# The fifth global transpose moved ahead of the FFN's second product, and other buffers for the last tokens

## The chip, the core and the metric

The kernel runs on one core of one Trainium2 chip. The metric is the device time of one execution in microseconds. Below, PE is TensorE, PEld its weight loads, DVE is VectorE, ACT is ScalarE, POOL is GpSimd and SP is SyncE, which here issues nearly all DMAs. L with a number is a line of the kernel.

## The reference, cut to what matters

Eight batches of eight heads: 512 local tokens attend to a window of 32 tokens on either side and to 32 global tokens; the 32 global tokens attend to all 544. Then a feed-forward network (FFN) over all 4608 tokens.

```python
# batch 8, heads 8, seq_l 512, seq_g 32, head_dim 64; d_model 512, d_ff 2048
s_g = scale * q_g @ [k_g, k_l]^T;  out_g = softmax(s_g) @ [v_g, v_l]
s_l = scale * [q_l @ k_g^T, where(|i-j| <= 32, q_l @ k_l^T, -1e9)]
out_l = softmax(s_l) @ [v_g, v_l]
x = concat(out_g, out_l) as (tokens, heads * head_dim)
h = x @ w_in;  r = max(h, 0);  y = (s * r * r + b) @ w_out
```

## The kernel before, in words

One loop over steps j runs everything as a pipeline. Step j takes one head of one half (256 tokens) of one batch: 16 steps make a batch, 128 steps make the attention. The FFN follows ten steps behind (LAG): with m = j - 10, `ffn_in(m)` makes 256 hidden columns for one tile of 256 tokens (24 matmuls, L508), and `ffn_out(m - 1)` multiplies the result of the step before with `w_out` (12 matmuls, L540, in two halves i = 0 and 1 of six each). Each float32 matrix is held as a high and a low part, so a product is made of three matmuls, and each evacuation from PSUM is a copy on ACT (high part) and a subtraction on DVE (low part).

The order within a step, in program order: split of the next keys and queries, loads, scores of head j (`scores`: L366 for the local ones, L370 for the global rows, then the softmax), transposes of the probabilities of head j - 1 (L312) interleaved with the products of head j - 2 (L391), `x_split` of a finished tile every eighth step, `ffn_in`, the entries of `extra`, and `ffn_out`. From step 20 on (ORDERED) the order on PE is exactly this program order; before it, and on all other engines and the DMA queues throughout, a planner chooses the order from its own estimate of when instructions become ready.

The global tokens: their scores are gathered over a batch in two tiles `sg` of four heads each (group g = 0 and 1). `g_softmax` runs at step 16b + 12 for g = 0 and 16b + 16 for g = 1. Three steps later (16b + 15 and 16b + 19) comes `g_transposes`, here called a turn: five 128x128 transposes of the 544 columns (L439), four into one PSUM tile with tag t and one into a tile with tag g, each followed by a copy on ACT (L442) and a subtraction on DVE (L443) into `pg`. `g_pv` (L460) uses `pg` one and three steps later, and stores its rows to a DRAM buffer `xg_d` (L469).

PSUM tags have one buffer each, so writers wait for the readers of the tile before. Tag t is shared by the probability transposes L312 of every step, the block of four in a turn, and the first transposes of `xg_split`. Tag g is shared by the global scores L370 of every step, the lone fifth transpose in a turn, and `g_pv`.

After the last head, the 256 global rows are the seventeenth tile of tokens: `xg_split(16)`, at m = 127 (step 137), loads them back from `xg_d` in two loads (L488), transposes them (L491) and splits them. Its two load buffers are of tag r, a ring of two that the FFN's hidden tiles `r` (L513) and output tiles `o` (L549) also use.

`ffn_out` is called with the turn as a function `between` and calls it between its two halves.

Of the kernel before, what the change touches and what calls it, by code (L numbers as in the profile page):

```python
# [10 lines left out]
F32 = mybir.dt.float32  # L11
# [9 lines left out]
DM, DF = 512, 2048  # L21
P = 128
HALF = 256
# [7 lines left out]
NC = 416  # L31
# [26 lines left out]
G_TR = 3  # L58
# [6 lines left out]
def f32(ap):  # L65
    return ap.bitcast(F32)
# [3 lines left out]
def window_attention_then_ffn(ctx: ExitStack, tc: tile.TileContext, qd, qg, kw, vw, vg, w_in, w_out, sv, bv, out):  # L70
# [4 lines left out]
    sb = ctx.enter_context(tc.tile_pool(name="sb", bufs=2))  # L75
# [89 lines left out]
    def slot(j):  # L165
        return j // 16, (j // 8) % 2, j % 8
# [66 lines left out]
    def own(k, hf):  # L233
        n, c = (192, P) if hf == 0 else (240, 144)
        return k[:, 0:2 * n].rearrange("p (k c) -> p k c", k=2)[:, :, 0:c]

    def sg_rows(j):
        b, hf, h = slot(j)
        if hf == 0 and h % 4 == 0:
            st_["sg", b, h // 4] = sb.tile([P, SGW], F32, tag=f"sg{h // 4}", name=f"sg{j}", bufs=1)  # L240
        r0 = 32 * (h % 4)
        return st_["sg", b, h // 4][r0:r0 + 32]

    def x_tile(j):
        b, hf, h = slot(j)
        t = 2 * b + hf
        if h == 0:
            xcur[t] = sb.tile([P, 4, HALF], F32, tag="x", name=f"x{t}", bufs=1)
        return xcur[t]

    def load32(j):
        b, hf, h = slot(j)
        if h % 2 == 0:
            if j % 4 == 0:
                rk = sb.tile([P, 480], F32, tag="rk", name=f"rk{j}", bufs=1)
            else:
                rk = sb.tile([P, 10 * D], F32, tag="rvg", name=f"rk{j}", bufs=1)[:, 0:480]
            nc.sync.dma_start(rk[:, 0:NC], kw[b, hf, h // 2])
            st_["rk", j] = st_["rk", j + 1] = rk
        if j % 2 == 0:  # L260
            rq = sb.tile([P, HALF], F32, tag="rq", name=f"rq{j}", bufs=1)
        else:
            rq = sb.tile([P, 288], F32, tag="tg", name=f"rq{j}", bufs=1)[:, 0:HALF]
        nc.sync.dma_start(rq, qd[b, hf, h])
        st_["rq", j] = rq

# [89 lines left out]
    def scores(j):  # L356
        b, hf, h = slot(j)
        ks, qs = st_.pop(("ks", j)), st_.pop(("qs", j))
        p_s = ps.tile([P, 512], F32, tag="s", name=f"ps_s{j}")
        p_g = ps.tile([P, 512], F32, tag="g", name=f"ps_g{j}")  # L360
        qgh = st_["qgs", b][:, h]
        ng = 256 + 32 * hf
        for blk in range(2):
            cols = COLS[hf, blk]
            for a in range(2):
                nc.tensor.matmul(  # L366
                    p_s[:, cols], lhsT=qs[:, a, blk * P:(blk + 1) * P], rhs=ks[:, cols], start=(a == 0), stop=(a == 1),
                )
                if blk == hf and a == 0:
                    nc.tensor.matmul(p_g[0:64, 0:ng], lhsT=qgh, rhs=own(ks, hf), start=True, stop=True)  # L370
        softmax(j, p_s)

        tg = sb.tile([P, 288], F32, tag="tg", name=f"tg{j}", bufs=1)
        nc.scalar.copy(out=tg[0:32, 0:ng], in_=p_g[32:64, 0:ng])  # L374
        nc.vector.tensor_add(out=sg_rows(j)[:, hf * 256:hf * 256 + ng], in0=p_g[0:32, 0:ng], in1=tg[0:32, 0:ng])

# [7 lines left out]
    xcur = {}  # L384
# [47 lines left out]
    def g_transposes(b, g):  # L432
        sg = st_["sg", b, g]
        pg = st_["pg", b, g] = sb.tile([P, 5, 4, 2, SG], F32R, tag="pg", name=f"pg{b}_{g}", bufs=1)
        for c0, c1, tag in ((0, 4, "t"), (4, 5, "g")):
            p_t = ps.tile([P, 4, P], F32, tag=tag, name=f"ps_tg{b}_{g}_{c0}")
            for c in range(c0, c1):
                s0 = min(c * P, SGW - P)
                nc.tensor.transpose(out=p_t[:, c - c0, :], in_=sg[:, s0:s0 + P], identity=ident)  # L439
            v = p_t[:, 0:c1 - c0].rearrange("p c (h q) -> p (c h) q", h=4)  # L440
            ph, pl = (pg[:, c0:c1, :, i, :].rearrange("p c h q -> p (c h) q") for i in range(2))
            nc.scalar.copy(out=ph, in_=v)  # L442
            nc.vector.tensor_sub(out=pl, in0=v, in1=f32(ph))  # L443

    def g_load(b, h):
        rv = sb.tile([P, 10 * D], F32, tag="rvg", name=f"rvg{b}_{h}", bufs=1)
# [37 lines left out]
    def xg_split(t):  # L484
        xs = sb.tile([P, 2, 4, HALF], F32R, tag="xs", name=f"xs{t}", bufs=2)
        for i in range(2):
            xr = sb.tile([P, DM], F32, tag="r", name=f"xgr{i}", bufs=2)
            nc.sync.dma_start(xr, xg_d[i * P:(i + 1) * P, :])  # L488
            p_t = ps.tile([P, 4, P], F32, tag="ts"[i], name=f"ps_xg{i}")
            for c in range(4):  # L490
                nc.tensor.transpose(out=p_t[:, c, :], in_=xr[:, c * P:(c + 1) * P], identity=ident)  # L491
            q = slice(i * P, (i + 1) * P)
            nc.scalar.copy(out=xs[:, 0, :, q], in_=p_t)
            nc.vector.tensor_sub(out=xs[:, 1, :, q], in0=p_t, in1=f32(xs[:, 0, :, q]))
        xs_[t] = xs
# [31 lines left out]

    oacc = {}

    def ffn_out(m, between=None):  # L530
        t, pr = m // 8, m % 8
        g = gs_.pop(m)
        if pr == 0:
            oacc[t] = [ps.tile([P, DM], F32, tag=f"acc{i}", name=f"acc{t}_{i}") for i in range(2)]
        for i in range(2):
            n = 0
            for k in range(2):
                f = 2 * pr + k
                for a, e in ((0, 0), (0, 1), (1, 0)):
                    nc.tensor.matmul(  # L540
                        oacc[t][i], lhsT=g[:, a, k, i * P:(i + 1) * P], rhs=wo[:, e, f, :],
                        start=(pr == 0 and n == 0), stop=(pr == 7 and n == 5),
                    )
                    n += 1
            if i == 0 and between:
                between()
        if pr == 7:
            for i in range(2):
                o = sb.tile([P, DM], F32, tag="r", name=f"o{t}_{i}", bufs=2)  # L549
                nc.scalar.copy(out=o, in_=oacc[t][i])  # L550
                if t < 16:
                    b, hf = t // 2, t % 2
                    r0 = b * (SL + SG) + SG + hf * HALF + i * P
                    nc.sync.dma_start(out[r0:r0 + P, :], o)
                else:
                    rows = out.rearrange("(b r) d -> b r d", r=SL + SG)[4 * i:4 * i + 4, 0:SG, :]
                    nc.sync.dma_start(rows, o)
# [5 lines left out]
    extra, turns = defaultdict(list), {}  # L563
    for b in range(B):
        for g in range(2):
            s0 = 16 * b + G_AT[g]
            extra[s0].append(lambda b=b, g=g: g_softmax(b, g))
            turns[s0 + G_TR] = lambda b=b, g=g: g_transposes(b, g)
            for i in range(2):
                h = 4 * g + 2 * i  # L570
                extra[s0 + G_TR + G_LD[i]].append(lambda b=b, h=h: g_load(b, h))
                extra[s0 + G_TR + G_PV[i]].append(lambda b=b, h=h: g_pv(b, h))
# [22 lines left out]
    for j in range(NM + LAG + 2):  # L595
        if j == ORDERED:
            fixed.enter_context(tc.manual_schedule(engines={mybir.EngineType.PE}))
        sp(j + 1)
        ld(j + 2)
        vl(j)  # L600
        for _ in range(PIECES[j] if j < len(PIECES) else 0):
            weight_piece(piece)
            piece += 1
        if j < NS:
            b1 = j // 16 + 1
            if j == 14 and NF > 16:
                qg_load32(1)
            elif j % 16 == 14 and b1 < B:
                qg_load(b1)
            sc(j)  # L610
            if j == NF - 1 and NF % 16:
                if NF > 16:
                    qg_load(j // 16)
                qg_split(j // 16)
            if j % 16 == 15 and NF <= j + 1 < NS:
                qg_split(b1)
        tr(j - 1)
        transposes_and_pv(j - 1, j - 2)
        vsp(j - 1)
        pvs(j - 2)  # L620
        vl32(j)
        m = j - LAG
        if j % 8 == 1 and 9 <= j <= NS + 1:
            x_split(j // 8 - 1)
        if m == 8 * 16 - 1:
            xg_split(16)
        if 0 <= m < NM:
            ffn_in(m)
        for fn in extra.pop(j, []):
            fn()  # L630
        if 0 <= m - 1 < NM:
            ffn_out(m - 1, turns.pop(j, None))
        elif j in turns:
            turns.pop(j)()
    fixed.close()
    assert piece == 32 and not extra

# [67 lines left out]
```

## Time and profile before

| | us |
|---|---|
| median of 3 runs | 1074.07 (1072.61 to 1075.57) |
| profiled execution | 1072.88 |
| its span, first to last instruction | 1071.1 |
| PE busy | 1031.5 |
| DVE busy | 823.1 |
| ACT busy | 707.4 |

The span is what the profile's views cover; the rest of the execution's time lies around it. A busy engine is not always doing useful work at its peak: matmuls are pipelined and their ends are modelled, so starts are compared below and not ends. Idle time of an engine matters only where it is on the chain that ends last.

### The profile page before, as it was taken

To read this page: it belongs to the slowest core of one execution; us is meant where nothing else is said; L and a number is where in the kernel's file an instruction comes from. 1 tells how busy PE (TensorE), PEld (TensorE's weight loads), DVE (VectorE), ACT (ScalarE), POOL (GpSimd) and SP (SyncE) were. 2 spreads that over 40 slices of the span, in tenths; PEclk is the share of its full clock that TensorE was granted. 3 is DMA by queue.
4 is the path that set the end of the run, shared out by engine and by line. 5 is a ranking of instruction groups with operands and counts; after the bars stand their busy time and mean duration, and the time that the engine had idled before them with its cause. 6 is when DMAs were issued, how large, how long until landed. Compare 5 with 4: busy or idle time off the path is not lost.

```text
span 1071.1 us, 20557 instructions
## 1 busy us (share of the span) xinstructions
PE 1031.5 (96%) x7076; PEld 923.2 (86%) x7076; DVE 823.1 (77%) x2116; ACT 707.4 (66%) x1796; POOL 328.5 (31%) x397
## 2 busy tenths in 40 slices
PE   6989999999999999999999999999999999999896
PEld 2558888999899989999899989998999989999895
DVE  6798778788888878888888888887888878863221
ACT  4677767677777777777667776777677776643221
POOL 3132534234333333234333343233333333211000
PEclk7569999999999999999999999999999999999998
DMA  7665332222222222213222132212221221101000
GB/s 241 192 207 191 97 101 80 67 66 64 90 74 71 64 84 74 76 57 95 67 73 71 58 101 65 76 57 83 88 76 53 79 81 56 59 13 34 21 21 20
DMA packets 63536, 86.80 MB, mean 81 GB/s; under 512 B 7624, under 2 KB 50632, under 8 KB 63432
## 3 DMA queue, kind: packets, MB, share of 16 engines
q1 hardware_dynamic: 63144, 84.44, 25.5%
q8 instruction: 56, 0.92, 0.3%
q10 hardware_dynamic: 288, 1.05, 0.3%
q14 instruction: 48, 0.39, 0.1%
HBM read 76.02 MB, written 9.44 MB: 80 GB/s over the span
## 4 chain that ended last, share of the span: by engine, by line
PE 79%; DVE 11%; ACT 4%; DMA 3%; issue 2%; POOL 0%; SPq 0%; DVEq 0%; ACTq 0%
PE ps_h L508 31%; PE acc L540 30%; PE ps_t L312 4%; PE ps_s L366 4%; PE ps_o L391 4%; DMA wst<-in_w_in 2%; PE ps_og L460 2%; PE ps_g L370 1%; DVE g L523 1%; PE ps_o L328 1%; PE ps_s L282 1%; DVE r L515 1%; DVE x L404 1%; DVE pg L443 1%; DVE sm L227 1%
## 5 line engine op out<-in xcount | busy, mean ns | idle before, releaser
L508 PE MATMUL ps_h<-xs,wi 128*128 128x256 f32 x3264 | 426.0, 286 | 0.0
L508 PEld LDWEIGHTS ps_h<-xs,wi 128*128 128x128 f32 x3264 | 402.2, 190 | 4.8 <-ACT pt L319 0.9
L540 PE MATMUL acc<-wo,g 128*128 128x512 f32 x1632 | 403.6, 393 | 0.9 <-ACT g L522 0.9
L540 PEld LDWEIGHTS acc<-wo,g 128*128 128x128 f32 x1632 | 295.3, 188 | 55.9 <-ACT g L522 1.1
L523 DVE SCALAR_TENSOR_TENSOR g<-r,b_t,g 128x512 fp32r<-128x512 f32 x136 | 118.7, 873 | 72.6 <-ACT g L522 71.9
L522 ACT ACTIVATE g<-r,b_t 128x512 fp32r<-128x512 f32 x136 | 98.5, 724 | 102.8 <-DVE r L515 102.4
L192 POOL TENSOR_TENSOR kq<-rk,kq 64x416 fp32r<-64x416 f32 x56 | 60.9, 1088 | 271.2 <-ACT kq L191 265.6
L515 DVE SCALAR_TENSOR_TENSOR r<-ps_h,s_t,r 128x512 f32<-128x512 f32 x136 | 101.2, 744 | 54.7 <-ACT r L514 54.6
L514 ACT ACTIVATE r<-ps_h 128x512 f32<-128x512 f32 x136 | 81.1, 596 | 93.6 <-PE ps_h L508 86.7
L194 POOL TENSOR_TENSOR kq<-rq,kq 128x256 fp32r<-128x256 f32 x112 | 84.4, 754 | 153.3 <-ACT kq L193 138.0
L220 ACT ACTIVATE sm<-sm,nm 128x224 f32<-128x224 f32 (+1 forms) x256 | 119.6, 469 | 1.7 <-DVE nm L214 1.3
L202 POOL TENSOR_TENSOR vs<-rv,vs 128x256 fp32r<-128x256 f32 x112 | 90.9, 812 | 52.4 <-ACT vs L201 45.8
L214 DVE CUSTOM_DVE_ANT_0 sm<-ps_s,mask 128x224 f32<-128x224 f32 (+1 forms) x256 | 85.6, 370 | 27.4 <-PE ps_s L366 15.4
L312 PE MATMUL ps_t<-ident,sm 128*128 128x128 f32 (+1 forms) x512 | 99.4, 279 | 4.9 <-POOL sm L227 4.8
L391 PE MATMUL ps_o<-pt,vs 128*128 128x256 f32 x448 | 90.6, 284 | 0.0
L374 ACT COPY tg<-ps_g 32x256 f32<-32x256 f32 (+1 forms) x112 | 42.2, 377 | 68.8 <-PE ps_g L370 66.5
L452 POOL TENSOR_TENSOR vsg<-rvg,vsg 128x320 fp32r<-128x320 f32 x64 | 56.3, 900 | 75.1 <-ACT vsg L451 75.1
L366 PE MATMUL ps_s<-kq 128*128 128x192 f32 (+1 forms) x448 | 78.4, 265 | 0.0
L366 PEld LDWEIGHTS ps_s<-kq 128*128 128x128 f32 x448 | 71.9, 189 | 6.8
L402 DVE TENSOR_TENSOR u<-ps_o,u 128x256 f32<-128x256 f32 x112 | 47.4, 423 | 34.0 <-ACT u L401 31.7
L404 DVE TENSOR_TENSOR x<-u 64x256 f32<-64x256 f32 x112 | 69.1, 617 | 3.8
L312 PEld LDWEIGHTS ps_t<-ident,sm 128*128 128x128 f32 (+1 forms) x512 | 59.2, 146 | 13.6 <-POOL sm L227 7.7
(79 smaller groups left out, 1278.1 us busy)
## 6 DMA issues: line engine op xcount, KB each, us to landing
rq<-in_qd SPq DMA_DIRECT2D x128, 128.0 KB, 2.2
rv<-in_vw SPq DMA_DIRECT2D x128, 128.0 KB, 2.0
rk<-in_kw SPq DMA_DIRECT2D x64, 208.0 KB, 2.4
rvg<-in_vg SPq DMA_DIRECT2D x32, 320.0 KB, 2.9
out<-o SPq DMA_DIRECT2D x34, 256.0 KB, 2.0
wst<-in_w_in SPq DMA_DIRECT2D x15, 512.0 KB, 4.7
wst<-in_w_out SPq DMA_DIRECT2D x15, 512.0 KB, 4.6
rqg<-in_qg SPq DMA_DIRECT2D x8, 128.0 KB, 2.5
```

The lines of the kernel that those rows point to most:

```text
L194: nc.gpsimd.tensor_sub(out=qs[:, 1, :], in0=rq, in1=f32(qs[:, 0, :]))
L202: nc.gpsimd.tensor_sub(out=vs[:, :, 1, :], in0=rv4, in1=f32(vs[:, :, 0, :]))
L214: nc.vector.tensor_tensor_reduce(out=sm[:, c], in0=p_s[:, c], in1=mask, op0=ALU.add, op1=ALU.min, scale=-scale, scalar=BIG, accum_out=nm[: ...
L220: nc.scalar.activation(out=p, in_=p, func=AF.Exp, bias=nm[:, blk:blk + 1], scale=-1.0, accum_out=ss[:, blk:blk + 1],)
L312: nc.tensor.transpose(out=p_t[:, at:at + q], in_=sm[0:q, c0:c0 + P], identity=ident[0:q, 0:q])
L366: nc.tensor.matmul(p_s[:, cols], lhsT=qs[:, a, blk * P:(blk + 1) * P], rhs=ks[:, cols], start=(a == 0), stop=(a == 1),)
L391: nc.tensor.matmul(p_o[:, blk, :, q0:q0 + n], lhsT=vs[:, 2 * blk + c], rhs=pt[:, :, o], start=(c == 1), stop=(c == 0),)
L508: nc.tensor.matmul(p_h[:, k], lhsT=wi[:, a, c, f * P:(f + 1) * P], rhs=xs[:, e, c, :], start=(n == 0), stop=(n == 11),)
L515: nc.vector.scalar_tensor_tensor(out=r, in0=p_h, scalar=s_t, in1=r, op0=ALU.mult, op1=ALU.mult)
L522: nc.scalar.activation(out=g[:, 0], in_=r, func=AF.Identity, bias=b_t)
L523: nc.vector.scalar_tensor_tensor(out=g[:, 1], in0=r, scalar=b_t, in1=f32(g[:, 0]), op0=ALU.add, op1=ALU.subtract,)
L540: nc.tensor.matmul(oacc[t][i], lhsT=g[:, a, k, i * P:(i + 1) * P], rhs=wo[:, e, f, :], start=(pr == 0 and n == 0), stop=(pr == 7 and n == 5),)
```

## The change

`g_transposes` becomes a generator with a pause after each of its two blocks, and its blocks change places: first the lone fifth transpose with its copy and subtraction (tag g), then the block of four (tag t). `ffn_out` advances it once ahead of each half. So the fifth transpose now stands between `ffn_in` and `ffn_out`, and the block of four stays between the halves. In `xg_split` the two load buffers are cut from tiles of tag pt (the ring of two for transposed probabilities, 832 columns each) instead of tag r. The tile `x` grows by 24 columns (96 bytes in each partition), and the tiles of tag tg by 40 columns (160 bytes); nothing reads or writes the added columns.

```diff
     def x_tile(j):
...
-            xcur[t] = sb.tile([P, 4, HALF], F32, tag="x", name=f"x{t}", bufs=1)
+            x = sb.tile([P, 4 * HALF + 24], F32, tag="x", name=f"x{t}", bufs=1)
+            xcur[t] = x[:, 0:4 * HALF].rearrange("p (c q) -> p c q", c=4)
...
-            rq = sb.tile([P, 288], F32, tag="tg", name=f"rq{j}", bufs=1)[:, 0:HALF]
+            rq = sb.tile([P, 328], F32, tag="tg", name=f"rq{j}", bufs=1)[:, 0:HALF]
...
-        tg = sb.tile([P, 288], F32, tag="tg", name=f"tg{j}", bufs=1)
+        tg = sb.tile([P, 328], F32, tag="tg", name=f"tg{j}", bufs=1)
...
     def g_transposes(b, g):
...
-        for c0, c1, tag in ((0, 4, "t"), (4, 5, "g")):
+        for c0, c1, tag in ((4, 5, "g"), (0, 4, "t")):
...
             nc.scalar.copy(out=ph, in_=v)
             nc.vector.tensor_sub(out=pl, in0=v, in1=f32(ph))
+            yield
...
     def xg_split(t):
...
-            xr = sb.tile([P, DM], F32, tag="r", name=f"xgr{i}", bufs=2)
+            xr = sb.tile([P, 2 * NC], F32, tag="pt", name=f"xgr{i}")[:, 0:DM]
...
-    def ffn_out(m, between=None):
+    def ffn_out(m, turn):
...
         for i in range(2):
+            next(turn, None)
...
-            if i == 0 and between:
-                between()
...
-            turns[s0 + G_TR] = lambda b=b, g=g: g_transposes(b, g)
+            turns[s0 + G_TR] = g_transposes(b, g)
...
-            ffn_out(m - 1, turns.pop(j, None))
-        elif j in turns:
-            turns.pop(j)()
+            ffn_out(m - 1, turns.pop(j, iter(())))
+        else:
+            list(turns.pop(j, ()))
```

## Rows read from the trace of the kernel before

**Rows 1.** The page's busy line (share of span), and its chain by engine.

```profile
PE 1031.5 (96%) x7076; PEld 923.2 (86%) x7076; DVE 823.1 (77%) x2116; ACT 707.4 (66%) x1796; POOL 328.5 (31%) x397
...
PE 79%; DVE 11%; ACT 4%; DMA 3%; issue 2%; POOL 0%; SPq 0%; DVEq 0%; ACTq 0%
```

**Rows 2.** The table of waits: who waited for whom, us, times, longest.

```profile
PEld ps_g L370 <- DVE pg L443: 10.6, 7, 1.5
...
PE ps_g L370 <- DVE pg L443: 9.7, 13, 1.2
```

**Rows 3.** Timeline, an ordinary step: start, us, engine, line, operation, [idle before <-releaser].

```profile
255.69 0.25 PE L366 MATMUL ps_s<-kq 128*128 128x192 f32 x1
...
255.78 0.28 PE L370 MATMUL ps_g<-kq,qgs 128*64 128x256 f32 x1
...
256.44 0.47 PE L312 MATMUL ps_t<-ident,sm 128*128 128x128 f32 x3
```

**Rows 4.** Timeline, a long turn (step 35) and the next step's scores.

```profile
274.45 1.56 PE L540 MATMUL acc<-wo,g 128*128 128x512 f32 x6
...
275.85 0.77 PE L439 MATMUL ps_tg<-ident,sg 128*128 128x128 f32 x5
...
276.37 1.64 PE L540 MATMUL acc<-wo,g 128*128 128x512 f32 x6
276.96 0.73 ACT L522 ACTIVATE g<-r,b_t 128x512 fp32r<-128x512 f32 x1 [1.67 <-DVE r L515]
277.59 0.73 ACT L442 CAST pg<-ps_tg 128x512 fp32r<-128x512 f32 x2
...
277.72 0.75 DVE L523 SCALAR_TENSOR_TENSOR g<-r,b_t,g 128x512 fp32r<-128x512 f32 x1 [0.79 <-ACT g L522]
277.85 0.25 PE L366 MATMUL ps_s<-kq 128*128 128x192 f32 x1
278.39 0.88 DVE L443 TENSOR_TENSOR pg<-ps_tg,pg 128x512 fp32r<-128x512 f32 x2
...
279.32 0.33 PE L370 MATMUL ps_g<-kq,qgs 128*64 128x256 f32 x1 [1.22 <-DVE pg L443]
...
280.01 0.49 PE L312 MATMUL ps_t<-ident,sm 128*128 128x128 f32 x3
```

**Rows 5.** Timeline, a short turn (step 31) and the next step's scores.

```profile
245.79 0.71 PE L439 MATMUL ps_tg<-ident,sg 128*128 128x128 f32 x5
...
246.42 0.76 ACT L442 CAST pg<-ps_tg 128x512 fp32r<-128x512 f32 x2 [0.90 <-PE ps_tg L439]
...
247.15 0.88 DVE L443 TENSOR_TENSOR pg<-ps_tg,pg 128x512 fp32r<-128x512 f32 x2
...
247.73 0.25 PE L366 MATMUL ps_s<-kq 128*128 128x192 f32 x1
...
248.18 0.31 PE L370 MATMUL ps_g<-kq,qgs 128*64 128x256 f32 x1 [0.20 <-DVE pg L443]
```

**Rows 6.** Groups by line and shape: count, busy us, mean ns, idle before.

```profile
L443 DVE TENSOR_TENSOR pg<-ps_tg,pg 128x512 fp32r<-128x512 f32 x16 | 10.9, 682 | 0.0
...
L443 DVE TENSOR_TENSOR pg<-ps_tg,pg 128x128 fp32r<-128x128 f32 x16 | 4.5, 280 | 0.0
```

**Rows 7.** The chain that ended last, by time: start, us, what.

```profile
1005.10 2.67 DMA xgr<-xg_d
...
1007.81 0.66 PE ps_xg L491 x4
```

**Rows 8.** SP's queue: one wait of the loads, then its timeline from 980 to 1010.

```profile
SPq L488 <- DVE g L523: 6.8, 1, 6.8
...
980.61 11.81 SPq L469 DMA_DIRECT2D xg_d<-xr  x2
999.27 6.17 SPq L488 DMA_DIRECT2D xgr<-xg_d  x2
```

**Rows 9.** One line's matmuls: duration in ns, shortest/median/longest, first and last start.

```profile
L540 PE MATMUL acc<-wo,g x1632: 387/389/504, 95.1 to 1061.7; 128*128 128x512 f32 x182
```

## The prediction

> **What bounds the kernel now.** I read the page's busy line first: PE is busy for 96% of the span, DVE for 77%, ACT for 66% [rows 1]. The chain that ended last is 79% PE [rows 1]. So time can only be won where PE stands still, or by doing fewer matmuls; the change does not alter the number of matmuls. Next I read the table of waits for PE and PEld, and looked only at the names that the diff touches. PE waits 13 times in front of L370, the global scores, for DVE L443: 9.7 us in all. PEld waits at the same place 7 times, 10.6 us, so 1.5 us each [rows 2]; these two rows overlap in time and are not added. Sixteen turns (the steps with global transposes) exist; step 15 lies where the planner still orders PE, and steps 127 and 131 are followed by no scores, which leaves 13: seven long ones (steps 16b+19) and six short ones (16b+15, b from 1). 7 x 1.22 + 6 x 0.20 = 9.7 agrees with [rows 2, 4, 5].
>
> Then the timeline of one ordinary step and one turn of each kind. In the ordinary step the first scores matmul L366 starts at 255.69, L370 at 255.78, and the first transpose of the probabilities, L312, at 256.44: 0.09 and 0.75 us after L366 [rows 3]. After the long turn the same three start at 277.85, 279.32 and 280.01, that is 1.47 and 2.16 us after L366 [rows 4]. The loss is 2.16 - 0.75 = 1.41 us. After the short turn L370 starts 248.18 - 247.73 = 0.45 us after L366, a loss of 0.36 us [rows 5]. Why: bank g holds the fifth transpose, is its turn's last piece of work, and L370 writes the same bank. In the long turn the order on ACT is g (L522) and then both copies L442; on DVE it is g (L523) and then both subtractions L443, ending at 278.39 + 0.88 = 279.27. PE starts 0.05 us later.
>
> **Part 1, the fifth transpose goes first.** It now runs at the place where ffn_out begins, 274.45 in the long turn [rows 4], ahead of six L540, and the other four stay between the halves. No instruction is added or removed: PE has the same matmuls, ACT the same two copies, DVE the same two subtractions, and no DMA is in this part. Bank g's tenant before it, the step's own global scores, was written a whole `ffn_in` of 24 matmuls earlier, so PE should not wait there. The copy of 128 columns is ready for ACT by 275.2 at the latest, even if the one transpose took the 0.71 us of five [rows 5]. Before L522 ACT stands idle for 1.67 us, waiting for DVE L515 [rows 4], so the copy costs nothing. Without that idle it would delay L522 by its own length, under half of the 0.73 us of both copies. The subtraction (0.28 us) is ready before DVE's idle 0.79 us in front of L523 [rows 4], and fits into it; L523 then starts as before. So bank g is free by about 277.3, before L370 wants it at 277.85 + 0.09 = 277.94. That wait goes, by this reading, in all 13 places.
>
> What is late next? Bank t. The block of four keeps its place on all three engines: its copy stands behind L522 and its subtraction behind L523, from 278.39 on. It takes 0.68 us [rows 6] and ends at 279.07; with the 0.05 us above PE may write bank t at 279.12. But the transposes L312 of the next step want that bank at 277.85 + 0.75 = 278.60. So after a long turn PE waits 0.52 us at L312 instead of 1.41 us at L370: the gain is 0.89 us, seven times, 6.2 us. Behind that new wait on PE stand the other transposes, two products L391 and the next 24 L508; ACT L514 waits for these, but no later than it does now. After a short turn the order is the other one: copies ahead of L522 and subtractions ahead of L523, and the block's subtraction is over at 247.15 + 0.68 = 247.83 [rows 5, 6], before 247.73 + 0.75 = 248.48. Nothing takes the place of that wait: 6 x 0.36 = 2.2 us.
>
> Does a lone transpose cost more than one of five? In the turn five L439 last 0.77 us together, and the next L540 starts at 276.37, before they end at 275.85 + 0.77 = 276.62 [rows 4]. In the short turn the five take 0.71 us [rows 5]. So they are pipelined with what follows, and I take nothing for the split. The Trainium skill, page "TensorE: Matmul & The Clock Gate", section "Part 4: PE-mode transpose", gives about 275 ns for one transpose inside a kernel; a transpose that paid this alone, and not 0.71/5 = 0.14 us, would cost 16 x 0.13 = 2.1 us, and the sum by it, as an estimate, would be 9.0 us instead of 11.1. The overlap in these rows speaks against that reading.
>
> **Part 2, the last tokens' buffers.** xg_split reads the 256 global rows back through two buffers. They came from ring r, which the FFN's r and o tiles use; now they come from ring pt, which nobody uses after the last head. The load issued at 999.27 had waited 6.8 us in SP's queue for DVE L523, that is for a buffer of r, although the last store to xg_d was issued by 980.61 + 11.81 = 992.42 [rows 8]. The second load was late: PE stood still from 1005.10 to 1007.81, for that DMA's 2.67 us [rows 7]. From ring pt both loads can be issued once the store has landed; taking 2.67 us for that landing and as much for each load, one behind the other, they are there at 992.42 + 3 x 2.67 = 1000.4, four microseconds before PE asks. They pass nothing in SP's queue: between 992.42 and 999.27 it issues no other transfer. 2.7 us go, with bounds of 0 (loads no earlier) and 2.7 us; I take the upper one, because the wait in the queue is for the buffer and that reason is gone.
>
> **Part 3, two buffers grow.** No instruction reads the added bytes. What changes is where the tiles allocated behind them lie. No row shows what an address is worth, so I bound it by tiles that already rotate through different places: L540 reads g from two buffers, and its shortest and median matmul are 387 and 389 ns [rows 9]. Within 2 ns of 389 that is at most half a percent either way on 403.6 us, some 2 us; I take 0 and keep 2 us to either side. The turns of steps 15 and 19 lie where the planner orders PE too and may place the pieces otherwise; the nearest row is a long turn's loss of 1.41 us, so I keep 2 x 1.41 = 2.8 us to either side and take 0 beyond what is counted above.
>
> **The sum.** 6.2 + 2.2 + 2.7 = 11.1 us. The profiled execution took 1072.88 us, of which 1071.1 are its span; that gives 1061.8. The median of the runs shown is 1074.07, 1.2 us above it, and the forecast is made for a median: 1074.07 - 11.1 = 1063.0 us.
>
> **The rivals.**
> - *Both waits go.* The planner sets the order on ACT and DVE from its own clock. If it puts the block's copy ahead of L522 in the long turns too, as it already does in the short ones [rows 5], bank t is free in time, and the whole 1.41 us is won seven times: 9.9 + 2.2 + 2.7 = 14.8 us, 1059.3. For it: the 1.67 us of idle ACT would take that copy. Against: the block's transposes finish no earlier than before, so what made the planner choose stays.
> - *The orders turn out worse.* If the lone subtraction is put behind L523 (ended 277.72 + 0.75 = 278.47), bank g comes free at 278.75 and t at 279.43: from L366 to L312 1.63 us, a gain of 0.53 us, 3.7 + 2.2 + 2.7 = 8.6 us, 1065.5. If the short turns flip to the long ones' order, their gain becomes a loss of about 0.24 us each: 6.2 - 1.4 + 2.7 = 7.5 us, 1066.6. Against both: the lone piece is ready 1.5 us or more before L522.
> - *The change does not do what it says.* The planner leaves the lone copy behind L522 and its subtraction last, so that only the last tokens' 2.7 us are won: 1071.4, within what can be told from no change. Against: it picks by readiness, as the two kinds of turn show.
> - *Slower, through the addresses.* If the moved tiles made TensorE's reads slower, every one of 3264 + 1632 = 4896 FFN matmuls would pay. 11.1 us / 4896 = 2.3 ns each eat up the gain; from 3.0 ns on the kernel is over 0.3% slower, and 5 ns would give 1074.07 - 11.1 + 24.5 = 1087.5. Against it: the 2 ns spread between shortest and median [rows 9].
>
> **How the numbers follow.** Forecast 0.45, both waits gone 0.22, worse orders 0.15, not what it says 0.10, addresses 0.08. A difference under 0.3%, about 3.2 us, cannot be told from none in measurements of this kernel. Faster by more than that: 0.45 + 0.22 + 0.15 = 0.82; within: 0.10; slower: 0.08. The range goes from the second case less some 2 us for addresses, 1057.5, to 1070.5: the worse orders' 1066.6 with 2 us for addresses and most of the 2.8 us for the early turns. It ends just under the case that wins only the last tokens' wait; that one and the slower one are left out, 0.18 in all.
>
> **What would show each step.** Right: the wait of PE L370 for DVE L443 disappears from the table; a new one, PE or PEld L312 for DVE L443, shows seven times with about half a microsecond each; short turns lose nothing; the two ps_xg groups stand together with no DMA between them in the chain; ordinary steps take what they took. The forecast is wrong if L312 waits for nothing after long turns (then it is nearer 1059), if L370 still waits, if ordinary steps away from the turns become longer, or if the stretch ahead of step 20, where the planner also orders PE, changes its length.

## The result and the profile after

| | before | after |
|---|---|---|
| median of the runs, us | 1074.45 (1072.61 to 1075.57, 4 runs) | 1057.98 (1055.96 to 1059.14, 4 runs) |
| ratio, with its 95% interval | | 0.9846 (0.9825 to 0.9867) |
| span of the profiled execution, us | 1071.1 | 1055.7 |

The changed kernel takes 16.5 us less. 1063.0 was forecast; 1057.98 lies in the stated range, near its lower end.

In the changed kernel the lines below the edits have moved: L508 is now L510 (first product), L540 is L543 (second product), L370 is L371, L312 is L313, L442 and L443 (copy and subtraction of the turn) are L443 and L444, L515 is L517, L522 and L523 (copy and subtraction of g) are L524 and L525.

The page's first line, and its busy line, which answers to [rows 1]:

```profile
span 1055.7 us, 20552 instructions
...
PE 1024.7 (97%) x7076; PEld 918.0 (87%) x7076; DVE 826.2 (78%) x2116; ACT 706.3 (67%) x1796; POOL 329.1 (31%) x397
```

PE has the same 7076 matmuls and is busy for 6.8 us less. That is the first sign of something the forecast does not have: fewer waits shorten the span, but should leave the busy time of the same matmuls as it was.

The table of waits (who waited for whom, us, times, longest), answering to [rows 2]:

```profile
PEld ps_t L313 <- DVE pg L444: 4.1, 7, 0.7
PE ps_t L313 <- DVE pg L444: 2.9, 6, 0.5
...
PEld ps_g L371 <- DVE pg L444: 1.5, 1, 1.5
PE ps_g L371 <- DVE pg L444: 1.2, 1, 1.2
```

Of 13 waits at bank g one is left, and six waits of half a microsecond at bank t have come. The one that is left follows the turn of step 19, ahead of step 20, where the planner orders PE as well.

The long turn of step 35 in the timeline (start, us, engine, line, operation), answering to [rows 4]:

```profile
270.49 3.06 PE L510 MATMUL ps_h<-xs,wi 128*128 128x256 f32 x24
...
273.39 0.27 PE L440 MATMUL ps_tg<-ident,sg 128*128 128x128 f32 x1
...
273.41 1.65 PE L543 MATMUL acc<-wo,g 128*128 128x512 f32 x6
...
274.13 0.26 ACT L443 CAST pg<-ps_tg 128x128 fp32r<-128x128 f32 x1
...
274.90 0.60 PE L440 MATMUL ps_tg<-ident,sg 128*128 128x128 f32 x4
...
275.81 0.28 DVE L444 TENSOR_TENSOR pg<-ps_tg,pg 128x128 fp32r<-128x128 f32 x1
275.92 0.72 ACT L524 ACTIVATE g<-r,b_t 128x512 fp32r<-128x512 f32 x1 [1.53 <-DVE r L517]
276.55 0.57 ACT L443 CAST pg<-ps_tg 128x512 fp32r<-128x512 f32 x1
276.68 0.75 DVE L525 SCALAR_TENSOR_TENSOR g<-r,b_t,g 128x512 fp32r<-128x512 f32 x1 [0.60 <-ACT g L524]
276.73 0.25 PE L367 MATMUL ps_s<-kq 128*128 128x192 f32 x1
276.82 0.28 PE L371 MATMUL ps_g<-kq,qgs 128*64 128x256 f32 x1
...
277.35 0.68 DVE L444 TENSOR_TENSOR pg<-ps_tg,pg 128x512 fp32r<-128x512 f32 x1
...
278.09 0.52 PE L313 MATMUL ps_t<-ident,sm 128*128 128x128 f32 x3 [0.48 <-DVE pg L444]
...
278.69 1.53 PE L510 MATMUL ps_h<-xs,wi 128*128 128x256 f32 x11
```

This is the forecast's picture. The lone copy stands in ACT's idle time (which is 1.53 us and was 1.67), its subtraction in DVE's (0.60 left of 0.79), and L371 starts 0.09 us after L367 instead of 1.47. L313 starts 278.09 - 276.73 = 1.36 us after L367; it was 2.16 before and 0.75 in an ordinary step. It waits for the block of four, behind g on both engines. From one first product to the next this step takes 278.69 - 270.49 = 8.20 us. Before it took 280.57 - 271.52 = 9.05:

```profile
271.52 3.10 PE L508 MATMUL ps_h<-xs,wi 128*128 128x256 f32 x24
...
280.57 3.12 PE L508 MATMUL ps_h<-xs,wi 128*128 128x256 f32 x24
```

The chain that ended last, at the last tokens, answering to [rows 7]:

```profile
993.03 0.87 PE ps_xg L493 x8
```

Eight transposes in one piece, with no DMA between them. The stop is gone.

What the forecast does not have shows best in the last steps, which hold nothing but the FFN: 24 matmuls of the first product, 12 of the second. The chain there, first before, then after (start, us, what):

```profile
1022.59 2.76 PE acc L540 x12
1025.35 2.88 PE ps_h L508 x24
...
1028.23 2.76 PE acc L540 x12
1030.99 2.88 PE ps_h L508 x24
```

```profile
1024.46 2.75 PE acc L543 x12
1027.20 2.80 PE ps_h L510 x24
...
1030.01 2.75 PE acc L543 x12
1032.75 2.80 PE ps_h L510 x24
```

5.64 us a step have become 5.55, with no wait in either. The same 24 matmuls take 0.08 us less, 3 ns each, in steps that no moved instruction touches. The clock is no reason: the granted clock is 1.00, the higher of the two levels (2.4 GHz), in both stretches. Nor are the other engines: while the first product runs from 1025.35 before and from 1027.20 after, ACT and POOL are idle, and DVE is busy for 0.20 and 0.28 us of its time.

### The profile page after: what moved, and what is told of

It reads as the page before. It is cut to its first block, busy times and chain, and to the rows that moved or that the text cites. A ratio compares the mean times of both kernels' runs of the same rounds, so it can differ in the third digit from the quotient of the medians.

```text
span 1055.7 us, 20552 instructions
## 1 busy us (share of the span) xinstructions
PE 1024.7 (97%) x7076; PEld 918.0 (87%) x7076; DVE 826.2 (78%) x2116; ACT 706.3 (67%) x1796; POOL 329.1 (31%) x397
## 4 chain that ended last, share of the span: by engine, by line
PE 81%; DVE 9%; ACT 4%; DMA 2%; issue 2%; POOL 0%; SPq 0%; DVEq 0%; ACTq 0%
PE ps_h L510 32%; PE acc L543 31%; PE ps_t L313 5%; PE ps_s L367 4%; PE ps_o L392 3%; PE ps_og L462 1%; DVE g L525 1%; PE ps_o L329 1%; PE ps_s L283 1%; PE ps_g L371 1%; DMA wst<-in_w_in 1%; DVE x L405 1%; PE ps_g L289 1%; DVE r L517 1%; ACT g L524 1%
## 5 line engine op out<-in xcount | busy, mean ns | idle before, releaser
L510 PE MATMUL ps_h<-xs,wi 128*128 128x256 f32 x3264 | 419.6, 283 | 0.0
L543 PE MATMUL acc<-wo,g 128*128 128x512 f32 x1632 | 405.9, 395 | 0.8 <-ACT g L524 0.8
L510 PEld LDWEIGHTS ps_h<-xs,wi 128*128 128x128 f32 x3264 | 396.2, 189 | 4.8 <-issue 1.0
L543 PEld LDWEIGHTS acc<-wo,g 128*128 128x128 f32 x1632 | 294.8, 188 | 56.9 <-ACT g L524 1.0
L525 DVE SCALAR_TENSOR_TENSOR g<-r,b_t,g 128x512 fp32r<-128x512 f32 x136 | 120.6, 886 | 70.5 <-ACT g L524 70.3
L524 ACT ACTIVATE g<-r,b_t 128x512 fp32r<-128x512 f32 x136 | 98.3, 723 | 103.4 <-DVE r L517 103.2
L517 DVE SCALAR_TENSOR_TENSOR r<-ps_h,s_t,r 128x512 f32<-128x512 f32 x136 | 101.2, 744 | 53.4 <-ACT r L516 53.4
L313 PE MATMUL ps_t<-ident,sm 128*128 128x128 f32 (+1 forms) x512 | 99.6, 279 | 8.0 <-POOL sm L227 5.0
L367 PE MATMUL ps_s<-kq 128*128 128x192 f32 (+1 forms) x448 | 78.0, 265 | 0.0
L367 PEld LDWEIGHTS ps_s<-kq 128*128 128x128 f32 x448 | 71.7, 189 | 6.8
L313 PEld LDWEIGHTS ps_t<-ident,sm 128*128 128x128 f32 (+1 forms) x512 | 59.1, 145 | 17.7 <-POOL sm L227 7.0
L227 DVE TENSOR_SCALAR sm<-sm,ss 128x192 f32<-128x192 f32 (+1 forms) x224 | 68.0, 345 | 1.5
```

Of the source, the lines that this page charges most:

```text
L313: nc.tensor.transpose(out=p_t[:, at:at + q], in_=sm[0:q, c0:c0 + P], identity=ident[0:q, 0:q])
L367: nc.tensor.matmul(p_s[:, cols], lhsT=qs[:, a, blk * P:(blk + 1) * P], rhs=ks[:, cols], start=(a == 0), stop=(a == 1),)
L510: nc.tensor.matmul(p_h[:, k], lhsT=wi[:, a, c, f * P:(f + 1) * P], rhs=xs[:, e, c, :], start=(n == 0), stop=(n == 11),)
L517: nc.vector.scalar_tensor_tensor(out=r, in0=p_h, scalar=s_t, in1=r, op0=ALU.mult, op1=ALU.mult)
L524: nc.scalar.activation(out=g[:, 0], in_=r, func=AF.Identity, bias=b_t)
L525: nc.vector.scalar_tensor_tensor(out=g[:, 1], in0=r, scalar=b_t, in1=f32(g[:, 0]), op0=ALU.add, op1=ALU.subtract,)
```

## The experiments

Where a step's length is given without a row, it is the time from the first matmul of `ffn_in` to that of the next step; "ordinary" is the median over the steps from 31 to 119, "FFN-only" the mean over the last seven. The kernel before has 6.97 us in an ordinary step and 5.64 in an FFN-only one.

**The three parts, one at a time.** Each is the kernel before with one of the edits, or the changed kernel without one:

```diff
 e1_turn:    the changed kernel with
-x = sb.tile([P, 4 * HALF + 24], ...); tg, rq = sb.tile([P, 328], ...); xr = sb.tile([P, 2 * NC], F32, tag="pt", ...)
+x, tg, rq and xr as in the kernel before
 e2_load:    the kernel before with
+xr = sb.tile([P, 2 * NC], F32, tag="pt", name=f"xgr{i}")[:, 0:DM]
 e3_grow:    the kernel before with
+x = sb.tile([P, 4 * HALF + 24], ...); tg, rq = sb.tile([P, 328], ...)
 e4_nogrow:  the changed kernel with
-x = sb.tile([P, 4 * HALF + 24], ...); tg, rq = sb.tile([P, 328], ...)
+x, tg and rq as in the kernel before
```

Expected of e1_turn:

> Part 1 alone: the fifth transpose goes first; buffers and the last tokens' loads as before. Theory A (each part is worth what its own stretch shows, and the rest of the gain belongs to the buffers' addresses): 6 long turns x 0.86 and 6 short ones x 0.43, that is 7.7 us less than before; ordinary steps keep 6.94 us, FFN-only steps 5.64. Theory B (the turns are worth more than they show, since the relieved ACT and DVE speed up the ordinary steps behind them): 12 to 13 us less, and ordinary steps become shorter.

Expected of e2_load:

> Part 2 alone: the last tokens' rows are loaded into ring pt. Both theories: the 3.0 us stop between the two transposes of the last tokens goes, nothing else moves: 3 us less than before.

Expected of e3_grow:

> Part 3 alone: the two buffers grow, so the tiles behind them move by 160 bytes and, from r on, by 256; the instructions are those of before in the same order on every engine. Theory A: 4 to 5 us less, spread evenly over all steps (FFN-only steps 5.64 to 5.55 us, the spacing of the FFN's first matmuls 119.7 to 117 ns). Theory B: nothing, within 0.1%. The rival of the prediction (moved tiles make TensorE's reads slower) would give a longer time.

Expected of e4_nogrow:

> The changed kernel without part 3; its instructions and their order are those of the changed kernel. Theory A: about 10.8 us less than before and 5 us more than the changed kernel, FFN-only steps back at 5.64 us. Theory B: as fast as the changed kernel, 16 us less than before.

| kernel | median, us | less than before (1075.45) | ratio, 95% interval |
|---|---|---|---|
| e1_turn | 1067.82 | 7.6 | 0.9936 (0.9916 to 0.9956) |
| e2_load | 1072.43 | 3.0 | 0.9962 (0.9946 to 0.9979) |
| e3_grow | 1069.96 | 5.5 | 0.9950 (0.9933 to 0.9967) |
| e4_nogrow | 1065.38 | 10.1 | 0.9908 (0.9891 to 0.9924) |

The parts add up: 7.6 + 3.0 + 5.5 = 16.1, against 16.5 for all three. Theory A holds, theory B falls: growing two buffers that nobody reads in full is worth 5.5 us by itself, and without it the changed kernel is 10.1 us faster than before, not 16. The 5.5 is rough, its interval reaching from 3.5 to 7.2 us; from step 20 to step 145 the trace of e3_grow takes 4.3 us less than that of before (885.4 against 889.7). In e3_grow the instructions and their order on every engine are those of before, and all 13 waits at bank g are still there:

```profile
PEld ps_g L371 <- DVE pg L444: 10.6, 7, 1.5
PE ps_g L371 <- DVE pg L444: 10.1, 13, 1.2
```

Yet its FFN-only steps have the changed kernel's length; its chain near the end:

```profile
1028.57 2.75 PE acc L541 x12
1031.32 2.80 PE ps_h L509 x24
```

**Which tile's place?** In the program as compiled, part 3 moves the tiles from kq up to x by 160 bytes, and those from r on (g among them) by 256. Among the moved tiles are operands of matmuls everywhere: kq, vs and pt in the attention, xs as the moving operand of the first product. Two kernels part these, with an empty tile ahead of xs:

```diff
 e5_xs:    the changed kernel, tg, rq = sb.tile([P, 288], ...) as before, and ahead of the first xs
+            sb.tile([P, 40], F32, tag="gap", name="gap", bufs=1)
 e6_notxs: the changed kernel, x = sb.tile([P, 4, HALF], ...) as before, and ahead of the first xs
+            sb.tile([P, 24], F32, tag="gap", name="gap", bufs=1)
```

Expected of e5_xs:

> The changed kernel, but of the tiles only xs (the FFN's tokens, TensorE's moving operand in the first product) and x start 160 bytes later; kq, vs, pt and the others in front lie where they lay before, r and g 256 bytes later as in the changed kernel. The order of all instructions is the changed kernel's. Theory X (the start of xs decides): as fast as the changed kernel, 16 us less than before; FFN-only steps 5.55 us. Theory Y (the attention's tiles or several at once decide): 10 to 11 us less than before, as without part 3, FFN-only steps 5.64 us.

Expected of e6_notxs:

> The reverse: all tiles in front of xs start 160 bytes later, as in the changed kernel, and xs and all behind it 256 bytes later. Theory X with a period of 256 bytes or a divisor of it: 10 to 11 us less than before, FFN-only steps 5.64 us. Theory Y: 16 us less than before, ordinary steps as in the changed kernel.

e5_xs took 1058.57 us (16.2 less than the 1074.77 of before beside it; ratio 0.9846, 0.9816 to 0.9875), e6_notxs 1065.48 (9.3 less; 0.9919, 0.9896 to 0.9942). The start of xs gives the whole effect (x moves with it, but no matmul reads x), and these places of the other tiles give no gain: theory X. In e6_notxs, xs also lies 256 bytes further from wi than in e4_nogrow, and the FFN-only step is the same. The chains near the end, e5_xs first:

```profile
1027.02 2.75 PE acc L544 x12
1029.77 2.80 PE ps_h L511 x24
```

```profile
1025.96 2.76 PE acc L543 x12
1028.72 2.88 PE ps_h L510 x24
```

**Which place, and relative to what?** Three more shifts of the tiles from kq to x, each made up for by x so that r and g stay where the changed kernel has them, modulo 256; and one kernel in which all tiles from the weights wi on move together:

```diff
 e7_by64:    the changed kernel with
+tg, rq = sb.tile([P, 304], ...); x = sb.tile([P, 4 * HALF + 48], ...)
 e8_by128:   the changed kernel with
+tg, rq = sb.tile([P, 320], ...); x = sb.tile([P, 4 * HALF + 32], ...)
 e11_by192:  the changed kernel with
+tg, rq = sb.tile([P, 336], ...); x = sb.tile([P, 4 * HALF + 16], ...)
 e9_all64:   e4_nogrow with
+    const.tile([P, 16], F32, name="gap")
     wi = const.tile([P, 2, 4, DF], F32R, name="wi")
```

Expected of e7_by64:

> The changed kernel with 64 bytes in place of 160 for the tiles from kq to x (tg grows by 64, x by 192 bytes). Theory X64 (the start of xs within 64 bytes decides; 160 moves it by half of 64, 64 not at all): as without part 3, 10 to 11 us less than before, FFN-only steps 5.64 us. Theory X128 (within 128 bytes or more): a step of its own, different from 5.64 us.

Expected of e8_by128:

> The same with 128 bytes (tg and x grow by 128 each). Theory X64 and X128: as without part 3, FFN-only steps 5.64 us. Theory X256 (within 256 bytes, so that xs then starts on a multiple of 256 as wi does): a step of its own, different from 5.64 us.

Expected of e9_all64:

> The changed kernel without part 3, but every tile from the weights wi on, the weights included, starts 64 bytes later. xs then starts 192 bytes past a multiple of 256, as in the fastest layout so far, but its distance to wi (the stationary operand of the same matmuls) is that of the kernel without part 3. Theory D (the distance between the two operands decides): as without part 3, FFN-only steps 5.64 us, ordinary ones 6.97, 10 us less than before. Theory S (the start of xs itself decides): 5.55 and 6.92 us, 19 to 20 us less than before.

Expected of e11_by192:

> The tiles from kq to x start 192 bytes later (tg grows by 192, x by 64), so xs starts 64 past a multiple of 256. If only the distance to the multiples of 128 counts, as the four starts so far suggest (0 and 128 slow, 32 and 192 fast), this is as fast as with 64 bytes: 19 to 20 us less than before, FFN-only steps 5.55 us. If the place within 256 counts, it may lie anywhere between the slow starts (7 to 10 us less) and the fast one.

All kernels of this table have the instructions of the changed kernel in the same order. The distance is the start of xs less that of wi, modulo 256 bytes; the FFN-only step is split into its 24 matmuls of the first and its 12 of the second product:

| kernel | distance | FFN-only step, us | of it first, second product | ordinary step, us | median, us | ratio to before, 95% interval |
|---|---|---|---|---|---|---|
| e4_nogrow | 128 | 5.64 | 2.88, 2.76 | 6.97 | 1065.38 | 0.9908 (0.9891 to 0.9924) |
| e6_notxs | 128 | 5.64 | 2.88, 2.76 | 7.00 | 1065.48 | 0.9919 (0.9896 to 0.9942) |
| e9_all64 | 128 (xs itself at 192) | 5.64 | 2.88, 2.76 | 6.98 | 1064.01 | 0.9898 (0.9874 to 0.9922) |
| e8_by128 | 0 | 5.62 | 2.87, 2.75 | 6.99 | 1067.83 | 0.9937 (0.9912 to 0.9962) |
| e11_by192 | 64 | 5.59 | 2.83, 2.76 | 6.95 | 1059.16 | 0.9855 (0.9836 to 0.9874) |
| changed kernel | 32 | 5.55 | 2.80, 2.75 | 6.94 | 1057.98 | 0.9846 (0.9825 to 0.9867) |
| e7_by64 | 192 | 5.55 | 2.83, 2.72 | 6.92 | 1054.49 | 0.9814 (0.9791 to 0.9837) |

X64 falls: 64 bytes move the time by 10.9 us against e4_nogrow. Theory S falls with e9_all64: there xs starts where it does in e7_by64, the fastest of the table, but wi has moved along, and the steps are those of e4_nogrow. So the place of xs counts relative to the tiles that moved along in e9_all64. That the one of them that matters is wi, the other operand of the same matmul (theory D), is argued and not shown alone: wo, r and g moved along too. For it: in the FFN-only steps the first product's matmuls read only xs and wi, and the other engines are nearly idle while they run.

My guess for e11_by192, that only the distance from multiples of 128 counts, missed for the kernel: 64 and 192 differ by 4.7 us. In the FFN-only steps the first product takes 2.83 us with either, and 32 is the fastest place with 2.80; the 0.04 us between e11_by192 and e7_by64 is in the second product. In the 53 steps from 32 to 119 that hold scores but no work for the global tokens, the first product takes, from its first matmul to the second product's, a mean of 2.96 us with distance 0, 2.94 with 128 (e4_nogrow), 2.89 with 32, 2.88 with 64 and 2.84 with 192, while the attention's matmuls keep 1.27 to 1.28 us. So most of what the places give there is in the first product too, but in another order than in the FFN-only steps; why is open. Whether the distances 0 and 128 differ is not settled; their intervals overlap. The chains, e9_all64, then e11_by192, then e7_by64:

```profile
1027.04 2.88 PE ps_h L510 x24
1029.92 2.76 PE acc L543 x12
```

```profile
1026.94 2.76 PE acc L543 x12
1029.70 2.83 PE ps_h L510 x24
```

```profile
1022.31 2.83 PE ps_h L510 x24
1025.14 2.72 PE acc L543 x12
```

In e7_by64 it is the second product of these steps that became shorter too, though its own operands lie as in the changed kernel. Why is open.

**The rest of the long turn.** If the wait at bank t is there because the block of four stands behind g, then g behind the block should remove it. In e10_front (on e7_by64's layout) the last two instructions of `ffn_in` are issued after `ffn_out` in the long turns, with an order edge on ACT and on DVE:

```diff
-            ffn_in(m)
+            finish = ffn_in(m)
+            late = j in turns and j % 16 == 3 and j >= 20
+            if not late:
+                finish()
...
             ffn_out(m - 1, turns.pop(j, iter(())))
+            if late:
+                finish(st_["block"])
```

Expected:

> The layout by 64 bytes, and in the long turns g is made behind the block of four: on ACT the block's copy ahead of the copy of g, on DVE its subtraction ahead of that of g; PE's order is unchanged. Theory (the rest of the long turn's loss is the block's place behind g): the wait of the next transposes for the block goes, six long turns become 0.5 to 0.6 us shorter (8.2 to 7.6 us), 3 us less than with the layout alone. Rival (ACT or DVE is late there anyway, and g late makes the next second product wait): no gain, and a wait of the second product for g.

1050.40 us (1049.74 to 1051.96), 4.1 less than e7_by64 and 7.6 less than the changed kernel; ratio to before 0.9776 (0.9757 to 0.9795). It is the fastest kernel of this study. A long turn in its timeline:

```profile
276.93 0.60 PE L440 MATMUL ps_tg<-ident,sg 128*128 128x128 f32 x4
...
277.57 0.59 ACT L443 CAST pg<-ps_tg 128x512 fp32r<-128x512 f32 x1 [1.14 <-PE ps_tg L440]
277.85 1.03 DVE L443 TENSOR_TENSOR pg<-ps_tg,pg 128x128 fp32r<-128x128 f32 x2
278.05 0.73 ACT L519 ACTIVATE g<-r,b_t 128x512 fp32r<-128x512 f32 x1
278.76 0.26 PE L367 MATMUL ps_s<-kq 128*128 128x192 f32 x1
278.82 0.75 DVE L520 SCALAR_TENSOR_TENSOR g<-r,b_t,g 128x512 fp32r<-128x512 f32 x1
...
279.49 0.49 PE L313 MATMUL ps_t<-ident,sm 128*128 128x128 f32 x3
```

Both subtractions end at 278.88, and L313 starts 0.73 us after L367, as in an ordinary step. The long turns went from 8.22 to between 7.50 and 7.54 us: 6 x 0.7 = 4.2 us, which is the whole difference. Putting g behind cost nothing: its subtraction starts 278.82 - 276.93 = 1.89 us after the block's transposes, in the changed kernel 276.68 - 274.90 = 1.78, and PE waits for g in front of a second product once in either (0.7 and 0.8 us).

**Does the second product care too?** Its stationary operand is g, its moving one wo. e12_g64 moves g (and r, which no matmul reads) by 64 bytes:

```diff
 e10_front with
-x = sb.tile([P, 4 * HALF + 48], ...)
+x = sb.tile([P, 4 * HALF + 64], ...)
```

Expected:

> The kernel of e10_front with x grown by 64 bytes more, so that g (the stationary operand of the second product) and r start 64 bytes past a multiple of 256, while wo (its moving operand) stays on one: the moving operand is then 192 bytes ahead of the stationary one, as in the first product's fastest layout. Theory D2 (the distance between the operands decides in the second product too): the spacing of its matmuls in FFN-only steps, now 226.7 ns, changes by over 1 ns, and all steps with it, 2 us or more in all, and shorter if the same distances are good there. Rival (it matters only in the first product): the FFN-only step stays at 5.55 us and the time within 1.5 us of e10_front.

1054.92 us (ratio 0.9814, 0.9797 to 0.9830), 4.5 more than e10_front. Its chain near the end:

```profile
1028.72 2.79 PE acc L547 x12
1031.51 2.83 PE ps_h L509 x24
1034.34 2.80 PE acc L547 x12
1037.14 2.74 PE ps_h L509 x24
```

The twelve matmuls went from 2.72 us to 2.79 and 2.80: the place of g counts there as well, as theory D2 has it, and my guess of the good direction was wrong; 192 is not a good distance as such. That it counts by its distance from wo is not shown alone: ACT and DVE write r and g, which both moved, while the second product runs.

The same chain limits theory D. The first product's operands lie where they lay in e10_front, and its 24 matmuls take 2.83 us there; here they take 2.83 and 2.74 us in turn, though all tiles of neighbouring steps lie alike modulo 256. So the distance of a matmul's own operands modulo 256 does not settle its time alone. What else does is open.

## Why the prediction was right, and where a term was off

- **The fifth transpose first: right, mechanism and size.** For a long turn 0.89 us was forecast, with the wait moving to bank t; 9.05 - 8.20 = 0.85 came (8.22 in e1_turn, which has this part alone), and the wait is where it was said to be. For a short turn 0.36 was forecast; in e1_turn two of them went from 7.91 and 7.90 us to 7.55 and 7.53, that is 0.36 and 0.37 (in the changed kernel they take 7.48 and 7.47: the rest is the addresses). e1_turn as a whole gives 7.6 us where 6.2 + 2.2 = 8.4 was forecast, and e4_nogrow, which has the first two parts, 10.1 where the sum has 11.1.
- **The count of long turns: off by one.** Seven were counted, six gained. The turn of step 19 lies where PE's order is the planner's; it still has its 1.2 us. So the new wait of PE stands six times in the table, not seven. The text put that stretch in the range and not in the sum, which counted the turn as if it were ordered.
- **The split of the five transposes costs nothing: right.** From the lone transpose at 273.39 to the block at 274.90 there are 1.51 us; before, the six L540 ahead of the block took 1.40 [rows 4]. The lone one adds 0.11 us there, and the block has one transpose fewer. The Trainium skill, page "TensorE: Matmul & The Clock Gate", section "Part 4: PE-mode transpose", gives about 275 ns for one of bf16 in a kernel. As a duration the row at 273.39 agrees, with 0.27 us from start to end; it is not what the transpose adds, for the next matmul starts 0.02 us behind its start, at 273.41.
- **The last tokens' buffers: right.** 2.7 us forecast; e2_load alone gives 3.0, and there the step concerned went from 9.40 to 6.43 us (6.34 in the changed kernel).
- **The grown buffers: the term that was mis-sized.** 0, within 2 us either way, was taken; 5.5 came (e3_grow), and ordinary steps, which were to take what they took, went from 6.97 to 6.94 us, FFN-only ones from 5.64 to 5.55. The step that failed was the bound: the shortest and the median L540 differ by 2 ns [rows 9], and that was read as what an address is worth. But the two g buffers lie at the same place modulo 256, and so do the two xs buffers; the rotation never varied the place modulo 256 that the shifts above vary. And the bound was made on the second product, while the effect of this change was in the first. The rival that had this mechanism had it with one sign only, slower.
- **The rival "both waits go" gave 1059.3,** close to what was measured, for another reason than what happened: its wait at bank t did not go. Only the wait table and the lone e3_grow tell the two apart; the time does not. Its price was near, a little low: e10_front, which does what that rival says, won 0.7 us in each long turn where 0.52 was the loss worked out.
- **That the time lies in the range is partly luck.** It is inside by 0.5 us. The range's lower end was made of that rival's 1059.3 and some 2 us for addresses; the rival did not happen, and the addresses, with 5.5 us, took up its room.

## What to carry to other kernels

When one PSUM bank serves several purposes, its owner's last instruction on a slow engine is what the next matmul waits for: read the wait table for the bank's next writer, move the small piece into an engine's idle time, and then price the next bank in line before counting the whole wait as won. A buffer that grows or moves is an edit of the matmuls too: compare the matmul spacing in a stretch without waits, and measure the padding by itself before giving its effect to the edit beside it. Copies of a tile in a ring are no test of addresses unless their starts differ modulo the period in question.

## What the runs showed of the hardware

With the same instructions in the same order, the time of this kernel's float32 matmuls depends on where their operands start in SBUF. 24 matmuls of 128x256 took 2.88 us with the moving operand 128 bytes from the stationary one (modulo 256) and 2.80 us with 32; the whole kernel went from 1067.83 us (distance 0) to 1054.49 us (distance 192). Moving both operands by 64 bytes, with all tiles behind them, changed nothing in these steps (e9_all64), moving one with its neighbours did (e7_by64). The Trainium skill, page "SBUF — State Buffer", section "Who interferes with whom", calls TensorE's two read ports, for the moving operand and for the weights, independent. No run here looks at the ports; that a matmul's time would then not depend on its operands' places is not what these runs show. What in the memory makes the difference, what the period is (one shift by 256 bytes, in e6_notxs, changed nothing), and why each product's time moved with the other one's operands (e7_by64, e12_g64), stays open.

Runs of one kernel scatter by 2 to 9 us, and most of that seems to lie in the first steps: in the profiles of e4_nogrow, e6_notxs and e9_all64, which have the same instructions in the same order and the same distance, step 20 starts at 167.1, 164.5 and 158.7 us, while from there to step 145 they take 879.6, 881.0 and 879.5 us. So the last digit of a median here is not worth reading, and the step lengths are.
